# Halves of 128 tokens for the first FFN products of two units, and a wider choice of engine for conversions, in a local-attention and FFN kernel

## The chip, the cores and the metric

The kernel runs on one core of a Trainium2 chip. The core has TensorE (PE in the profile, its weight loads PEld), VectorE (DVE), ScalarE (ACT), GpSimd (POOL) and SyncE (SP), which here only issues DMAs. The metric is the device time of one execution in microseconds (us), lower is better.

## The reference

Attention over 4 batches, 8 heads, 768 tokens and 64 dimensions, in which each token sees its neighbours within 15 positions and, beside them, 24 block summaries (the maximum of the keys and the mean of the values of 32 tokens each); then an FFN over the 3072 resulting rows.

```python
k_sum = k.reshape(B, H, nb, 32, D).max(axis=3)
v_sum = v.reshape(B, H, nb, 32, D).mean(axis=3)
scores_l = where(|pos_i - pos_j| < 16, q @ k.T / sqrt(D), -1e9)
scores_s = q @ k_sum.T / sqrt(D) + log(32)
a = softmax(concat(scores_l, scores_s))          # over 768 + 24 keys
x = (a @ concat(v, v_sum)) as rows (3072, 512)
h = x @ w_in                                      # (3072, 2048)
g = h * sigmoid(h)
out = g @ w_out                                   # (3072, 512), float32
```

The inputs q and k are random with a spread of 0.8, v of 0.1. The FFN weights arrive as 64-bit floats.

## The kernel before, in words

**Tiling.** The 3072 rows are 24 stages of 128 tokens. Two stages make one chunk of 256 tokens, 12 chunks in all. The hidden dimension of 2048 is cut into 8 slices of 256, called f or fp. One FFN **unit** is a chunk with a slice; there are 96, numbered in the order in which they are worked (units 0 to 3 are chunk 0 with slices 0 to 3, units 4 to 7 chunk 1 with the same, then slices 4 to 7 of chunk 1, then of chunk 0, then the later chunks whole).

**A unit** (`job_f`) has two first products (`ffn1`, L904 to L908, d = 0 and 1), each 12 matmuls of 128x128 weights against 256 tokens, since x and the weights are held as a high and a low f16 part and three of the four cross terms are formed. Their result is in a PSUM bank h: 0 or 1 for the first chunks. Then ScalarE takes the tanh (L922), VectorE forms (t + 1) * h (L923), ScalarE casts that to f16 as gh (L927), and GpSimd or VectorE forms the rest gl = t - gh (L928, through the helper at L276). The first eight units that use slices 0 to 3 for chunks 0 and 1 are "plain": they have one scaled f32 copy g (L925) and no rest. The second products (L917) follow, 6 matmuls of 512 columns for each of the two halves of the tokens.

**A stage** (`job_a`, `job_c`, `job_x`): scores of two heads in one group (L671 for stages 0 to 3 in f32, L674 for 4 and 5, L676 and L677 later), a row minimum on VectorE (L688), the exponential with its sum on ScalarE (L691). In stages 0 to 3 the f32 exponentials are transposed on TensorE (L700, L702), copied out of PSUM by ScalarE or VectorE (L705), and multiplied with the values (L746, the AV product). A small product broadcasts the reciprocal sums (L791), VectorE multiplies (L795), and xh and xl, the two f16 parts of x, are formed (L797, L798). Later stages normalize first (L713, L715, L717), write two f16 parts, transpose them by DMA (L729) and multiply at L762.

**Weights** (`job_w`): each slice of w_in and w_out comes as 1 MB by DMA (L816), is rebuilt to f32 out of its two 32-bit words (L818 to L828), its largest value is found (L838, or as a bound by sums on ScalarE at L836 and L840), turned into a power of two with a small product (L848, L852), and split in two f16 parts: the high one on ScalarE (L860), the low one on VectorE (L861). The values' scale of batch 0 comes from VectorE maxima over six tiles (L603) in `job_mean`, which also forms the block means (L600).

**What sets the order.** Every operation is recorded in a `Plan` with the engines on which it may run, its cost there, and what it reads and writes. `ORDER` is a string in the program: each three characters, read to base 36, are the operation's number times five plus an engine's number (L182). `replay` (L178) runs through it, and the instructions of each engine are put out in that order; each engine works strictly in it. Since the list is plain text, it can be decoded by reading it against the numbers in which the program records its operations. Operations with the "port" mark on VectorE and GpSimd are kept from overlapping in the plan, and long GpSimd ones get a wait on the VectorE one before (L241).

**Fillers.** Where `replay` expects TensorE to stand idle early on, it puts in products of 256 columns with the identity (L389) that write to bank 0 and are not used. They end for good with the first operation that is entered with 3072 columns or more (L197), and that is the first `ffn1`.

**Queues.** All DMAs go out on SP, in their own order of `ORDER`.

Of the kernel before, what the change touches and what calls it, by code (L numbers as in the profile page):

```python
# [14 lines left out]
AF = mybir.ActivationFunctionType  # L15
ALU = mybir.AluOpType
# [5 lines left out]
P = 128  # L22
# [28 lines left out]
APART = 2  # L51
NSUP = 2
# [199 lines left out]
def local_attn_ffn(ctx: ExitStack, tc: tile.TileContext, q0, qkT, qF, qD, kF, kD, v, vR, w, out):  # L252
# [289 lines left out]
    def job_qk(s, prio):  # L542
# [22 lines left out]
        plan.op({"act": 1040}, lambda e: nc.scalar.activation(out=qh, in_=qr, func=AF.Copy, scale=qs[:, 0:1]), r=key + sc, w=[("qk", s % 2, hp) for hp in range(4)], prio=prio)  # L565
# [4 lines left out]
        plan.op({"act": 1240}, lambda e: nc.scalar.activation(out=kst[:, :, :NLOC], in_=kr, func=AF.Copy, scale=qs[:, 1:2]), r=key2 + sc, w=[("qkk", s % 2)], prio=prio)  # L570
# [16 lines left out]
    def job_mean(prio):  # L587
        prio += nudge("mean")
        k = sbank()
        for t in range(NTILE):  # L590
# [11 lines left out]
            if NPL < NTILE:  # L602
                plan.op({"dve": 603}, lambda e, src=src, t=t: nc.vector.tensor_reduce(out=am_t[:, t:t + 1], in_=src, axis=AX.X, op=ALU.max, apply_absolute_value=True), r=key, w=[("am", t)], prio=prio, port=())  # L603
# [5 lines left out]
    def job_vs(s, prio):  # L609
# [12 lines left out]
        def vm(e):  # L622
            for u in range(2):
# [3 lines left out]
        plan.op({"act": 1040, "pool": 1097}, lambda e: nc.scalar.activation(out=vr, in_=vr, func=AF.Copy, scale=vsc[:, 0:1]) if e == "act" else  # L627
                nc.gpsimd.tensor_scalar(out=vr, in0=vr, scalar1=vsc[:, 0:1], scalar2=0.0, op0=ALU.mult, op1=ALU.add), r=[("vsc", b % 2)], w=key, prio=prio)
# [141 lines left out]
    def job_x(s, prio):  # L770
# [7 lines left out]
        if s < NPL:  # L778
# [18 lines left out]
            plan.op({"act": 560}, lambda e: nc.scalar.copy(out=xh, in_=xr3), r=[("xr", s % 2)], w=[("xh", z, half)], prio=prio)  # L797
# [59 lines left out]
    def split_w(fp, kind, by, need, prio):  # L857
        wf = plain_w[fp, kind].rearrange("p j c -> p (j c)")
        hi, lo = (wt[fp, kind][:, i].rearrange("p j c -> p (j c)") for i in range(2))
        plan.op({"act": 1050}, lambda e: times(e, hi, wf, by), r=[("wv", fp, kind)] + need, w=[("wp", fp, kind), ("wh", fp, kind)], prio=prio)  # L860
# [29 lines left out]
    def job_f(i, c, f):  # L890
# [13 lines left out]
        def ffn1(d):  # L904
            def go(e):
                for ct in range(NCT):
                    for q, (part, x) in enumerate(((0, xh), (0, xl), (1, xh))):
                        nc.tensor.matmul(out=h[:, d * CH:(d + 1) * CH], lhsT=wt[f, 0][:, part, d, ct * P:(ct + 1) * P], rhs=x[:, ct, :], start=(ct == 0 and q == 0), stop=(ct == NCT - 1 and q == 2))  # L908
            return go
# [10 lines left out]
        for d in range(2):  # L920
# [3 lines left out]
        if plain:  # L924
            plan.op({"act": 600}, lambda e: times(e, g, t, ur_t[:, f, 0:1]), r=[("t", j), ("ur", f)], w=[("gh", n), ("gl", n)], prio=at - TUNE["post"])  # L925
# [245 lines left out]
```

## Time and profile before

| | |
|---|---|
| Median of 3 runs | 612.52 us (612.44 to 612.62) |
| Profiled execution | 612.63 us |
| its span, first to last instruction | 610.9 us |
| TensorE busy | 605.8 us, 99% |
| VectorE, ScalarE, GpSimd busy | 466.9, 391.5, 139.7 us |
| granted TensorE clock | 0.999 |
| DMA | 93.50 MB, mean 153 GB/s |

The span is what the trace shows, from the first instruction to the last; the rest of the execution's time, 1.7 us, lies around it. A product counts as busy from its issue until its modelled end, so that two in a row overlap: the step from one start to the next, not the length, is what a product costs in a row of them.

### The profile page before, as it was taken

To read this page: it belongs to the slowest core of one execution; us is meant where nothing else is said; L and a number is where in the kernel's file an instruction comes from. 1 tells how busy PE (TensorE), PEld (TensorE's weight loads), DVE (VectorE), ACT (ScalarE), POOL (GpSimd) and SP (SyncE) were. 2 spreads that over 40 slices of the span, in tenths; PEclk is the share of its full clock that TensorE was granted. 3 is DMA by queue.
4 is the path that set the end of the run, shared out by engine and by line. 5 is a ranking of instruction groups with operands and counts; after the bars stand their busy time and mean duration, and the time that the engine had idled before them with its cause. 6 is when DMAs were issued, how large, how long until landed. Compare 5 with 4: busy or idle time off the path is not lost.

```text
span 610.9 us, 13765 instructions
## 1 busy us (share of the span) xinstructions
PE 605.8 (99%) x5085; PEld 427.6 (70%) x5085; DVE 466.9 (76%) x1384; ACT 391.5 (64%) x866; POOL 139.7 (23%) x172
## 2 busy tenths in 40 slices
PE   8999999999999999999999999999999999999997
PEld 5786756677676776767777676767767667666785
DVE  7998978999889766897888846997788876753321
ACT  3999989667776667655787567644665655442222
POOL 2333321023314301413303341112422012101000
PEclk9999999999999999999999999999999999999999
DMA  8999615764666754583775764685565652502100
GB/s 310 342 335 382 248 40 167 172 158 114 191 137 141 202 172 142 158 210 82 195 145 130 173 194 136 152 197 124 98 161 130 143 131 64 87 14 57 53 2 35
DMA packets 91560, 93.50 MB, mean 153 GB/s; under 512 B 70348, under 2 KB 72652, under 8 KB 89444
## 3 DMA queue, kind: packets, MB, share of 16 engines
q1 hardware_dynamic: 91492, 92.62, 56.0%
q8 instruction: 40, 0.66, 0.5%
q14 instruction: 28, 0.23, 0.1%
HBM read 68.12 MB, written 6.29 MB: 122 GB/s over the span
## 4 chain that ended last, share of the span: by engine, by line
PE 94%; DMA 3%; ACT 1%; SPq 0%; DVE 0%; issue 0%
PE bank L917 42%; PE bank L908 41%; PE bank L762 4%; PE bank L676 2%; PE bank L677 2%; DMA wt<-in_w_dram 1%; DMA wt<-in_kF_dram 1%; PE bank L746 1%; DMA wt<-vms 1%; PE bank L674 1%; PE bank L671 0%; ACT wt L826 0%; ACT e L691 0%; PE bank L389 0%; PE bank L460 0%
## 5 line engine op out<-in xcount | busy, mean ns | idle before, releaser
L917 PE MATMUL bank<-wt,g 128*128 128x512 f16 (+2 forms) x1168 | 278.6, 382 | 0.0
L908 PE MATMUL bank<-xh,wt 128*128 128x256 f16 x1536 | 273.9, 273 | 0.0
L908 PEld LDWEIGHTS <-wt 128*128 128x128 f16 x2304 | 224.1, 98 | 45.1 <-issue 3.3
L908 PE MATMUL bank<-xl,wt 128*128 128x256 f16 x768 | 209.3, 273 | 0.0
L917 PEld LDWEIGHTS <-g 128*128 128x128 f16 x1104 | 106.7, 98 | 95.3 <-issue 0.8
L922 ACT ACTIVATE t<-bank,asc 128x512 f32<-128x512 f32 x96 | 65.7, 684 | 90.0 <-PE bank L908 89.7
L923 DVE SCALAR_TENSOR_TENSOR t<-t,bank 128x512 f32<-128x512 f32 x96 | 65.5, 683 | 55.7 <-ACT t L922 55.1
L691 ACT ACTIVATE e<-e,mx 128x182 f32<-128x182 f32 x192 | 83.8, 438 | 29.2 <-DVE mx L688 28.9
L927 ACT CAST g<-t 128x512 f16<-128x512 f32 x88 | 54.1, 615 | 49.4 <-DVE t L923 46.3
L726 DVE SCALAR_TENSOR_TENSOR p<-e,sum,p 128x128 f16<-128x128 f32 x320 | 80.1, 313 | 2.9 <-POOL p L715 1.7
L276 POOL TENSOR_TENSOR g<-t,g 128x512 f16<-128x512 f32 x31 | 35.9, 1158 | 161.3 <-ACT g L927 77.5
L688 DVE CUSTOM_DVE_ANT_0 e<-bank,masks,qsc 128x182 f32<-128x182 f32 x144 | 54.0, 402 | 21.0 <-PE bank L677 19.0
L715 POOL TENSOR_SCALAR p<-e,sum 128x182 f16<-128x182 f32 x45 | 24.6, 549 | 119.1 <-DVE sum L708 23.5
L276 DVE TENSOR_TENSOR g<-t,g 128x512 f16<-128x512 f32 x57 | 39.7, 696 | 12.0 <-ACT g L927 11.3
L691 ACT ACTIVATION_READ_ACCUMULATOR e<-e,mx 128x1 f32 x192 | 36.1, 188 | 0.0
L713 ACT ACTIVATE p<-e,sum 128x182 f16<-128x182 f32 x65 | 26.6, 437 | 14.1 <-DVE sum L708 7.4
L276 POOL TENSOR_TENSOR vv<-raw,vv 128x1024 f16<-128x1024 f32 x12 | 25.6, 2133 | 15.6 <-DVE p L717 5.9
L571 DVE SCALAR_TENSOR_TENSOR qk<-raw,qsc,qk 64x1264 f16<-64x1264 f32 x18 | 27.6, 1535 | 2.0 <-ACT qk L570 1.4
L676 PE MATMUL bank<-qk 128*128 128x182 f16 x144 | 28.7, 241 | 0.0
L677 PE MATMUL bank<-qk 128*128 128x182 f16 x144 | 28.7, 242 | 0.0
L570 ACT ACTIVATE qk<-raw,qsc 128x1264 f16<-128x1264 f32 x18 | 24.1, 1340 | 5.1 <-DMA raw<-in_kD_dram 5.1
L566 DVE SCALAR_TENSOR_TENSOR qk<-raw,qsc,qk 128x1024 f16<-128x1024 f32 x18 | 23.7, 1316 | 3.7 <-ACT qk L565 3.6
(169 smaller groups left out, 640.1 us busy)
## 6 DMA issues: line engine op xcount, KB each, us to landing
wt<-in_w_dram SPq DMA_DIRECT2D x16, 1024.0 KB
raw<-in_kD_dram SPq DMA_DIRECT2D x18, 632.0 KB
raw<-in_v_dram SPq DMA_DIRECT2D x20, 512.0 KB
raw<-in_qD_dram SPq DMA_DIRECT2D x18, 512.0 KB
out_dram<-raw SPq DMA_DIRECT2D x23, 256.0 KB
raw<-in_kF_dram SPq DMA_DIRECT2D x12, 384.0 KB
raw<-in_qF_dram SPq DMA_DIRECT2D x9, 512.0 KB
raw<-in_vR_dram SPq DMA_DIRECT2D x12, 384.0 KB
```

The costliest lines, as they stand in the source:

```text
L276: eng[e].tensor_tensor(out=out, in0=in0, in1=in1, op=ALU.subtract)
L571: plan.op({"dve": 1450}, lambda e: nc.vector.scalar_tensor_tensor(out=kst[64:, :, :NLOC], in0=kr[64:], scalar=qs[64:, 1:2], in1=kst[64:, : ...
L676: nc.tensor.matmul(out=sc[:, i, :NKEY], lhsT=qh[:, h, :], rhs=kst[:, h, :], start=True, stop=False)
L677: nc.tensor.matmul(out=sc[:, i, :NKEY], lhsT=ql[:, h, :], rhs=kst[:, h, :], start=False, stop=True)
L688: plan.op({"dve": 258 if b == 0 else 323}, lambda e, i=i: nc.vector.tensor_tensor_reduce(out=et[:, i, :NKEY], in0=sc[:, i, :NKEY], in1=mas ...
L691: plan.op({"act": 431}, lambda e, i=i, h=h: nc.scalar.activation(out=et[:, i, :NKEY], in_=et[:, i, :NKEY], func=AF.Exp, scale=-1.0, bias=m ...
L726: nc.vector.scalar_tensor_tensor(out=pt[:, i, to:to + z - a], in0=et[:, i, a:z], scalar=su[:, i:i + 1], in1=pt[:, i, a:z], op0=ALU.mult, o ...
L908: nc.tensor.matmul(out=h[:, d * CH:(d + 1) * CH], lhsT=wt[f, 0][:, part, d, ct * P:(ct + 1) * P], rhs=x[:, ct, :], start=(ct == 0 and q == ...
L917: nc.tensor.matmul(out=bank[to][:, :z0 - a0], lhsT=a[:, d * CH + u * P:d * CH + u * P + P], rhs=b[:, d, a0:z0], start=(opens and d == 0 an ...
L922: plan.op({"act": 640}, lambda e: nc.scalar.activation(out=t, in_=h, func=AF.Tanh, scale=asc_t[c // 3 % 2][:, f:f + 1]), r=[("bank", k), ( ...
L923: plan.op({"dve": 605}, lambda e: nc.vector.scalar_tensor_tensor(out=t, in0=t, scalar=1.0, in1=h, op0=ALU.add, op1=ALU.mult), r=[("bank", ...
L927: plan.op({"act": 540}, lambda e: nc.scalar.copy(out=gh, in_=t), r=[("t", j)], w=[("gh", n)], prio=at - TUNE["post"])
```

## The change

It has three parts, and a new `ORDER` (2532 entries in place of 2528).

**1. Halves.** For units 0 and 1 (chunk 0, slices 0 and 1) each of the two first products is made in two operations of 128 tokens each. One reads only the xh and xl of its own half of the chunk, that is, of one stage. There are eight operations of 12 matmuls with 128 columns where there were four of 12 with 256. Each is entered in the plan with 3072 columns, as a whole one.

**2. ScalarE may bound the values' scale by sums.** The reductions at L603 may run on ScalarE as a sum of absolute values, scaled by 2^-7, which writes its unused result to a buffer of the FFN. In the new order two of six do.

**3. Conversions may change engine.** Seven kinds of operation that had ScalarE alone, or ScalarE and GpSimd, may run on ScalarE, GpSimd or VectorE. What the new order makes of it, decoded:

| operation | count | moved |
|---|---|---|
| g cast to gh (L927) | 88 | 27 to GpSimd, 29 to VectorE |
| plain g (L925) | 8 | 3 to GpSimd, 2 to VectorE |
| high part of the weights (L860) | 16 | 7 to GpSimd |
| q (L565), k (L570) | 18 each | 2 and 3 to GpSimd, 1 and 2 to VectorE |
| xh of the first stages (L797) | 4 | 2 to GpSimd, 1 to VectorE |
| rest gl (L928) | 88 | 16 from GpSimd to VectorE, 13 the other way |
| scaled v (L627), its rest (L630) | 20 each | 6 from GpSimd to ScalarE and 2 to VectorE; 7 from GpSimd to VectorE |
| scaled exponentials (L713, L715, L717) | 160 | 102 change among the three |

In all VectorE has 958 operations instead of 926, ScalarE 594 instead of 642, GpSimd 164 instead of 148.

```diff
+HALVED = 2
@@ job_qk, split_w and others alike
-        plan.op({"act": 1040}, lambda e: nc.scalar.activation(out=qh, in_=qr, func=AF.Copy, scale=qs[:, 0:1]), ...)
+        plan.op({"act": 1040, "pool": 1110, "dve": 650}, lambda e: times(e, qh, qr, qs[:, 0:1]), ...)
@@ job_mean
+                def bound(e, src=src, t=t):
+                    if e == "act":
+                        nc.scalar.activation(out=t_t[t % NT2], in_=src, func=AF.Abs, scale=2.0 ** -7, accum_out=am_t[:, t:t + 1])
+                    else:
+                        nc.vector.tensor_reduce(out=am_t[:, t:t + 1], in_=src, axis=AX.X, op=ALU.max, apply_absolute_value=True)
+                plan.op({"dve": 603, "act": 620}, bound, r=key, w=[("am", t), ("t", t % NT2)], prio=prio, port=())
@@ job_f
-        def ffn1(d):
+        def ffn1(d, half=None):
+            a0, z0 = (0, CH) if half is None else (half * P, half * P + P)
...
-                        nc.tensor.matmul(out=h[:, d * CH:(d + 1) * CH], lhsT=..., rhs=x[:, ct, :], ...)
+                        nc.tensor.matmul(out=h[:, d * CH + a0:d * CH + z0], lhsT=..., rhs=x[:, ct, a0:z0], ...)
...
+        early = c == 0 and f < HALVED
+        for half in range(2 if early else 0):
+            for d in range(2):
+                plan.op({"pe": 690}, ffn1(d, half), r=[(x, z, half) for x in ("xh", "xl")] + ..., cols=3072)
+        for d in range(0 if early else 2):
...
-            plan.op({"act": 540}, lambda e: nc.scalar.copy(out=gh, in_=t), ...)
+            plan.op({"act": 540, "pool": 590, "dve": 345}, lambda e: copy(e, gh, t), ...)
```

TensorE's order around the first units, decoded (s is the stage, u the unit, "turn" the transposes of two heads, "sums" L791, "AV" L746, "gather" L848):

```
before: scores s2a | sums s1 | AV s1 | turn turn | gather | sums s2 | scores s3a | AV s2 |
        u0 d0 | turn turn | u0 d1 | scores s3b | u1 d0 | u1 d1 | second products of u0 ...
after:  sums s1 | scores s2a | gather | AV s1 | turn | u0 d0 tokens 0-127 | turn | sums s2 |
        u0 d1 tokens 0-127 | scores s3a | AV s2 | u0 d0 tokens 128-255 | turn turn |
        u0 d1 tokens 128-255 | u1 d0 tokens 0-127 | scores s3b | u1, three more | second products of u0 ...
```

(Here s2a stands for the second score group of stage 2, s3a and s3b for the two of stage 3.) The other orders are new throughout as well. On SP the first weights of slice 0 stand two places earlier, the last tile of v for the block means three places later.

More of the change, by code (lines that the diff above doesn't have):

```diff
@@ L564, in job_qk @@
         plan.op({"dma": 1360}, lambda e: nc.sync.dma_start(out=stg[:, :H * P], in_=qD[b - 1, t]), w=key, prio=prio)
-        plan.op({"act": 1040}, lambda e: nc.scalar.activation(out=qh, in_=qr, func=AF.Copy, scale=qs[:, 0:1]), r=key + sc, w=[("qk", s % 2, hp) for hp in range(4)], prio=prio)
+        plan.op({"act": 1040, "pool": 1110, "dve": 650}, lambda e: times(e, qh, qr, qs[:, 0:1]), r=key + sc, w=[("qk", s % 2, hp) for hp in range(4)], prio=prio)
         plan.op({"dve": 1200}, lambda e: nc.vector.scalar_tensor_tensor(out=ql, in0=qr, scalar=qs[:, 0:1], in1=qh, op0=ALU.mult, op1=ALU.subtract), r=key + sc, w=[("qk", s % 2, hp) for hp in range(4)], prio=prio)
@@ L626, in job_vs @@
         plan.op({"dma": 480}, vm, r=["vms"], w=key, prio=prio, cols=1520)
[L627 to L628 removed]
+        plan.op({"act": 1040, "pool": 1097, "dve": 650}, lambda e: times(e, vr, vr, vsc[:, 0:1]), r=[("vsc", b % 2)], w=key, prio=prio)
         plan.op({"dve": 602, "act": 950, "pool": 1014}, lambda e: copy(e, v1, vr), r=key, w=[("v1", j), ("v1", j, "side")], prio=prio)
@@ L796, in job_x @@
             xr3 = xr.rearrange("p (c t) -> p c t", c=NCT)
-            plan.op({"act": 560}, lambda e: nc.scalar.copy(out=xh, in_=xr3), r=[("xr", s % 2)], w=[("xh", z, half)], prio=prio)
+            plan.op({"act": 560, "pool": 590, "dve": 345}, lambda e: copy(e, xh, xr3), r=[("xr", s % 2)], w=[("xh", z, half)], prio=prio)
             plan.op({"dve": 680, "pool": 1280}, lambda e: less(e, xl, xr3, xh), r=[("xr", s % 2), ("xh", z, half)], w=[("xl", z, half)], prio=prio)
@@ L907, in go @@
                     for q, (part, x) in enumerate(((0, xh), (0, xl), (1, xh))):
-                        nc.tensor.matmul(out=h[:, d * CH:(d + 1) * CH], lhsT=wt[f, 0][:, part, d, ct * P:(ct + 1) * P], rhs=x[:, ct, :], start=(ct == 0 and q == 0), stop=(ct == NCT - 1 and q == 2))
+                        nc.tensor.matmul(out=h[:, d * CH + a0:d * CH + z0], lhsT=wt[f, 0][:, part, d, ct * P:(ct + 1) * P], rhs=x[:, ct, a0:z0], start=(ct == 0 and q == 0), stop=(ct == NCT - 1 and q == 2))
             return go
@@ L918, in ffn2 @@
             return go
-        for d in range(2):
+        early = c == 0 and f < HALVED
+        for half in range(2 if early else 0):
+            for d in range(2):
+                plan.op({"pe": 690}, ffn1(d, half), r=[(x, z, half) for x in ("xh", "xl")] + [("wh", f, 0), ("wl", f, 0)] + ([("turn", i - APART)] if i >= APART else []), w=[("bank", k)], prio=at + nudge("f1", i), cols=3072)
+        for d in range(0 if early else 2):
             plan.op({"pe": 1310}, ffn1(d), r=[(x, z, half) for x in ("xh", "xl") for half in range(2)] + [("wh", f, 0), ("wl", f, 0)] + ([("turn", i - APART)] if i >= APART else []), w=[("bank", k)], prio=at + nudge("f1", i), cols=3072)
```

137 lines of the change are left out of this document (68 added, 69 removed).

## The prediction, before the run

> **What bounds the kernel now.** I read the page first, then the windows by stage, then the timeline of single instructions between 20 and 46 us. The page:
>
> ```profile
> span 610.9 us, 13765 instructions
> PE 605.8 (99%) x5085; PEld 427.6 (70%) x5085; DVE 466.9 (76%) x1384; ACT 391.5 (64%) x866; POOL 139.7 (23%) x172
> ...
> PE 94%; DMA 3%; ACT 1%; SPq 0%; DVE 0%; issue 0%
> ```
>
> TensorE is the bound: it is busy for 605.8 of 610.9 us and carries 94% of the chain that ended last. Time can therefore only come out of what TensorE does that is not the computation, or out of its gaps. The windows (length, then busy us of each engine with its instruction count, clock, DMA share, GB/s) say where that is:
>
> ```profile
> 6.00:21.00 15.00, 14.66 (x105) 8.57 (x104) 13.01 (x48) 10.52 (x38) 1.16 (x1) 1.00 1.02 374
> 21.00:28.00 7.00, 6.80 (x91) 6.03 (x91) 6.79 (x26) 6.71 (x17) 2.53 (x2) 1.00 0.89 290
> ...
> 39.00:600.00 561.00, 561.00 (x4669) 396.55 (x4668) 431.53 (x1251) 359.06 (x784) 127.10 (x147) 1.00 0.55 143
> ```
>
> From 39 to 600 us no gap is recorded. But busy is not useful: L389, the filler product that keeps the array working, counts as busy too. The same windows, for L389 alone:
>
> ```profile
> 21.00:28.00 7.00, 1.21 (x10) 1.04 (x11) 1.00 0.89 290
> 28.00:33.00 5.00, 0.61 (x4) 0.14 (x2) 1.00 1.02 410
> 33.00:36.00 3.00, 1.86 (x14) 1.30 (x14) 1.00 0.72 210
> 36.00:611.00 575.00, 0.00 (x0) 0.00 (x0) 1.00 0.54 142
> ```
>
> After 21 us every filler lies before 36 us (those ahead of 21 are the opening run, until the first scores can start). What they stand in for is seen in TensorE's timeline (start, length, line, shape, count):
>
> ```profile
> 27.18 1.15 PE L389 MATMUL bank<-ident 128*128 128x256 bf16 x9
> 28.25 0.55 PE L671 MATMUL bank<-wt,qk 64*128 64x158 f32 x4
> ...
> 33.39 0.60 PE L389 MATMUL bank<-ident 128*128 128x256 bf16 x4
> 33.91 0.64 PE L791 MATMUL bank<-unit,sh 128*64 128x128 f16 x16
> 34.48 1.27 PE L389 MATMUL bank<-ident 128*128 128x256 bf16 x10
> 35.68 0.55 PE L671 MATMUL bank<-wt,qk 64*128 64x158 f32 x4
> ...
> 36.79 2.12 PE L746 MATMUL bank<-wt 128*64 128x128 f32 x32
> 38.84 0.28 PE L908 MATMUL bank<-xh,wt 128*128 128x256 f16 x1
> ```
>
> From filler start to next real start: 28.25 − 27.18 = 1.07, 33.91 − 33.39 = 0.52 and 35.68 − 34.48 = 1.20 us, 2.79 us in three places. That is nearly all there is to win. TensorE waits here for the early attention stages (tokens 0 to 511), whose chain runs through ScalarE and VectorE, and the FFN cannot fill the holes because its first instruction (38.84) reads both token halves of chunk 0.
>
> **The change part by part.** (1) The halves. What they need is ready earlier:
>
> ```profile
> 26.98 1.27 DVE L273 SCALAR_TENSOR_TENSOR wt<-wt,ur 128x1024 f16<-128x1024 f32 x1
> ...
> 39.74 1.27 DVE L273 SCALAR_TENSOR_TENSOR wt<-wt,ur 128x1024 f16<-128x1024 f32 x1
> ```
>
> ```profile
> 29.65 1.16 POOL L276 TENSOR_TENSOR xl<-xr,xh 128x512 f16<-128x512 f32 x1 [0.15 <-ACT xh L797]
> ...
> 36.48 1.17 POOL L276 TENSOR_TENSOR xl<-xr,xh 128x512 f16<-128x512 f32 x1 [1.96 <-DMA raw<-vms]
> ```
>
> Weights of unit 0 are split by 26.98 + 1.27 = 28.25 and tokens 0 to 127 by 29.65 + 1.16 = 30.81; tokens 128 to 255 only by 37.65, and unit 1's weights by 41.01. So exactly two half products, those of unit 0 over tokens 0 to 127, can run in the holes, and the decoded new order places exactly these two ahead of the scores that started at 35.68 and of the AV product (L746 at 36.79): the first between two transposes, the second between L791 and the scores.
>
> Their price. Twelve 256-column products take 1.31 us (24 in 2.73, with overlap at the end); the weight loads in between and the smaller shape nearest to the new one:
>
> ```profile
> 43.62 2.73 PE bank L908 x24
> ```
>
> ```profile
> 181.56 2.42 PE L762 MATMUL bank<-tt,vv 128*64 128x128 f16 x80
> ```
>
> ```profile
> L908 PEld LDWEIGHTS <-wt 128*128 128x128 f16 x2304 | 224.1, 98 | 45.1 <-issue 3.3 <-DVE wt L828 0.3 <-POOL raw L628 0.2
> ```
>
> No row shows a 128-column product with 128 new weight columns. Lower bound: half of 109 ns (1.31/12), 55 ns, 0.66 us for twelve. Upper bound: the whole 98 ns of a weight load, were none overlapped, 1.18 us. L762 loads 64 weight columns for each of its 128-column products and two of them cover the array: 2 × 2.35/80 = 59 ns, 0.70 us for twelve (2.35 is 2.42 without the tail that the next instruction overlaps). I take 0.70. Behind AV, units 0 and 1 then need six halves, 6 × 0.70 = 4.20, where four whole ones stood, 4 × 1.31 = 5.24: −1.04 us (bounds 6 × 0.66 − 5.24 = −1.28 and 6 × 1.18 − 5.24 = +1.84).
>
> [...]
>
> (2) Where the AV product ends. It is behind the scores at 35.68, which wait for banks 4 and 5 to be copied out. Here the engine choices act: one of the two copies that ScalarE ran in a row (the 27.18 hole) goes to VectorE, the broadcast product L791 for stage 1 moves into that hole, and VectorE, 13.01 of 15 and 6.79 of 7 us busy in the windows above, loses two of these reductions to ScalarE:
>
> ```profile
> 16.52 1.27 DVE L603 TENSOR_REDUCE am<-wt 128x1 f32<-128x512 f32 x2
> ```
>
> as well as one 1.2 us maximum of unit 1's weights. Against that, ScalarE is itself full from 28 us on, and the first half product delays the transpose behind it, which frees bank 4. Bounds: gain at most what the holes hold beyond the two halves, 2.79 − 1.40 = 1.39; loss at most one half product, 0.70. I take −0.5: the copy in parallel saves about 0.5 us in the 1.07 us hole, and the rest of the chain neither gains nor loses.
>
> (3) Conversions to f16 that leave ScalarE: 56 of the 88 casts of g (27 to GpSimd, 29 to VectorE), 7 of 16 weight splits to GpSimd, a few of q, k, v and x. Prices:
>
> ```profile
> L262 DVE CAST vv<-raw 128x1024 f16<-128x1024 f32 x3 | 2.1, 691 | 1.4 <-ACT raw L627 1.4
> ```
>
> ```profile
> L260 POOL TENSOR_SCALAR vv<-raw 128x1024 f16<-128x1024 f32 x10 | 10.5, 1046 | 33.7 <-DVE g L276 16.0 <-ACT xh L266 8.8 <-DVE qk L566 5.1
> ```
>
> At half the size a g cast is about 0.35 to 0.42 us on VectorE and 0.52 to 0.63 on GpSimd. On ScalarE it is 0.62, seen with its whole chain at the end of the kernel:
>
> ```profile
> 600.14 0.69 ACT L922 ACTIVATE t<-bank,asc 128x512 f32<-128x512 f32 x1 [1.22 <-PE bank L908]
> 600.86 0.69 DVE L923 SCALAR_TENSOR_TENSOR t<-t,bank 128x512 f32<-128x512 f32 x1 [1.14 <-ACT t L922]
> 601.63 0.62 ACT L927 CAST g<-t 128x512 f16<-128x512 f32 x1 [0.81 <-DVE t L923]
> 602.28 0.69 DVE L276 TENSOR_TENSOR g<-t,g 128x512 f16<-128x512 f32 x1 [0.74 <-ACT g L927]
> ```
>
> The chain takes 602.97 − 600.14 = 2.83 us, 3.1 with its start. TensorE covers it with other work: first and second products stream 3072 columns alike, 1.31 us, and a score group of 728 columns by the same rate 0.31. In the new order the shortest cover is then 2 × 1.31 + 2 × 0.31 = 3.2 us (unit 16, both steps on VectorE: 3.1 − 0.62 + 0.4 = 2.9 needed); for a unit with both steps on GpSimd it is 4.2 (unit 12: 2 × 1.31 and two f32 score groups of some 0.8, below the 1.11 us of the larger group at 35.68; 3.1 − 0.62 + 0.6 − 0.69 + 1.16 = 3.6 needed). So I cost part 3 at nothing; without that cover it costs what the chain is late, as the third rival prices. VectorE gains 32 instructions net; it was 431.53 of 561 us busy.
>
> (4) The DMA order: unit 0's first weights go two places earlier, the last mean tile three later; the count is the same. The DMA engines are full until 21 us (1.02), so it only shifts landings. I cost it at nothing, between −0.5 and +0.3 (the sizes of the gaps at 6 to 28 us, 0.34 + 0.20).
>
> Sum: −1.04 − 0.5 = −1.5 us. The profiled execution took 612.63 (610.9 plus 1.7 around it), the median 612.52: 612.5 − 1.5 = **611.0 us**, 0.25% faster. A difference under 0.2%, 1.2 us, cannot be told from no change here.
>
> **The rivals.** *Everything is recovered.* VectorE's relief also pulls the whole early chain forward and all 2.79 us go, with the gaps of 0.54: 612.5 − 2.79 − 0.54 + 0.35 (eight halves at 0.70 against four at 1.31) = 609.5. For it: VectorE is 97% busy at 21 to 28 us. Against: the transfer of the block means and ScalarE, not VectorE alone, set those stages.
>
> *The holes only move.* TensorE takes its instructions in order; a half product that waits holds the transpose and the scores behind it, so bank 4 is freed later, its copies later, the next scores later. If each half delays that chain by its own 0.70, AV ends 1.40 later and the −1.04 is gone: 612.5 to 612.9. For it: xl of half 0 now passes three GpSimd steps (weight split, xh, xl), before only xl. Against: 30.81 leaves some 1 us before the first half product can start.
>
> *GpSimd is held up by VectorE, and the second products wait (slower).* The row that speaks for it:
>
> ```profile
> 25.16 1.35 POOL L268 TENSOR_SCALAR asc<-ur,vsc 128x1 f32<-128x1 f32 x1
> ```
>
> ```profile
> 25.25 1.21 DVE L828 SCALAR_TENSOR_TENSOR wt<-wt 128x1024 uint32<-128x1024 uint32 x1
> ```
>
> One element took 1.35 us on GpSimd, just as long as the VectorE instruction beside it. By the same count three units with both steps on GpSimd have 4.2, 4.6 and 4.6 us of cover (units 12, 58, 83) for 3.6. One hold of 1.2 us costs them 0.6 + 0.2 + 0.2 = 1.0; two holds cost 1.8 + 1.4 + 1.4, and two more units with 5.0 and 5.6 of cover 1.0 and 0.4, together 6.0. Between them, 3.5: 612.5 − 1.5 + 3.5 = 614.5. It decides where a hold exceeds the 0.6 us of spare cover. Against it: GpSimd ran such steps before too (29.65 above), and TensorE had no gap from 39 to 600 us.
>
> [...]
>
> *Weight loads set the pace of the halves*: +1.84 in place of −1.04, 613.8. Against it: 59 ns at L762.
>
> *The clock drops.* No filler can be issued once the first half product is out. At half clock for 3.4 us of work, 1.7 us are lost: 612.7. Against it: the windows show a granted clock of 1.00 with fillers at 12 to 62% of a stretch, and in the stretch without them two halves, two transposes, L791, scores and AV leave holes under 1 us.
>
> [...]
>
> **How the numbers follow.** Forecast 0.42, everything recovered 0.13, holes only move 0.22, GpSimd held up 0.15, weight loads 0.05, clock 0.03. The forecast's own range is 610.2 to 611.9, from −0.5 ± 0.8 in part 2. Leaving out half of the first rival's side below and two thirds of the GpSimd case above, 80% lie in 609.6 to 613.4. Faster by 0.2% (under 611.3): most of the forecast, 0.36, and all of the first rival, 0.13, with 0.02 of the others: 0.51. Same (611.3 to 613.7): 0.06 + 0.20 + 0.03 + 0.03 = 0.32. Slower: 0.17.
>
> **What would show it.** Two half products of about 0.70 us ahead of the AV product, fewer than ten fillers after 28 us, and the AV product ending near 38.3: parts 1 and 2. No TensorE wait on g after 40 us: part 3. A half product well over 0.8 us, a granted clock under 1.00, or waits of the second products on GpSimd would each make it wrong by the rival that names it.

## The result and the profile after

Slower. The changed kernel takes 616.32 us (median of 8, 613.97 to 618.30) against 612.64 for the kernel before: ratio 1.0055, 95% interval 1.0037 to 1.0074. The prediction was 611.0 with a range of 609.6 to 613.4. On a second chip (run e10 below) it is 614.47 against 612.81, 1.0027 [1.0013, 1.0041]. The chips differ by less for the kernel before (612.6 to 613.0 throughout), so below each kernel is compared with the runs of before made beside it. One number needs a word more: in five of these eight executions the mean granted clock is 0.997 or less (0.996 in the profiled one, which dips between 28 and 32 us), and these are in the medians.

The page of the changed kernel, profiled execution 618.3 us. It is the slowest of the eight, so the profile of e10, the same kernel at 615.73 us and without a dip of the clock, is set beside it where the two differ:

```profile
span 616.6 us, 13824 instructions
PE 606.4 (98%) x5114; PEld 427.3 (69%) x5114; DVE 490.2 (80%) x1416; ACT 360.6 (58%) x821; POOL 130.7 (21%) x188
...
PE 84%; DMA 8%; DVE 3%; SPq 2%; issue 1%; ACT 1%; POOL 1%; ACTq 0%; POOLq 0%; DVEq 0%
```

TensorE's idle time has doubled, from 610.9 − 605.8 = 5.1 to 10.2 us, and the chain that ended last now runs 8% through DMAs, where it had 3%. Windows (length, busy of each engine with its count, clock, DMA share, GB/s) say where:

```profile
6.00:21.00 15.00, 14.15 (x103) 8.23 (x102) 12.45 (x48) 11.24 (x42) 1.17 (x1) 1.00 0.99 362
21.00:28.00 7.00, 5.95 (x82) 4.92 (x80) 5.45 (x23) 5.22 (x12) 1.34 (x2) 1.00 0.87 327
28.00:33.00 5.00, 5.00 (x48) 3.73 (x49) 3.40 (x8) 3.92 (x8) 3.32 (x5) 0.66 1.03 347
39.00:100.00 61.00, 59.34 (x456) 41.14 (x454) 54.26 (x110) 56.45 (x96) 22.22 (x31) 1.00 0.62 222
400.00:500.00 100.00, 98.09 (x829) 68.38 (x827) 85.44 (x260) 54.01 (x133) 17.15 (x26) 1.00 0.57 135
```

Between 21 and 28 us TensorE is idle for 1.05 us (0.20 before), and ScalarE and VectorE, busy 6.71 and 6.79 of those 7 us before, now 5.22 and 5.45: they stand still too. The clock then falls to 0.66 for 5 us, 5 × 0.34 = 1.7 us of work; in windows of 0.5 us it is 0.52 from 28.5 us, 0.50 from 29 to 31.5, 0.56 from 31.5 and 1.00 from 32 on. Further on TensorE has gaps of 1.66 and 1.91 us, where it had none. Its waits, by line and releaser (us in total, times, longest):

```profile
PE bank L925 <- POOL g L269: 1.7, 1, 1.7
PE bank L925 <- POOL g L277: 1.7, 1, 1.7
```

In e10 these two are 1.2 and 0.5 us, and there is one of 0.8 us for a query tile.

**The first place: up to 41 us.** The loads on SyncE's queue, before and then after:

```profile
10.29 0.33 SPq L816 DMA_DIRECT2D wt<-in_w_dram  x1
...
12.50 0.33 SPq L548 DMA_DIRECT2D qk<-in_q_dram  x1
12.87 1.01 SPq L816 DMA_DIRECT2D wt<-in_w_dram  x2
```

```profile
8.54 0.33 SPq L822 DMA_DIRECT2D wt<-in_w_dram  x1
12.75 0.33 SPq L549 DMA_DIRECT2D qk<-in_q_dram  x1
13.12 0.43 SPq L598 DMA_DIRECT2D wt<-in_v_dram  x1
...
14.99 0.43 SPq L822 DMA_DIRECT2D wt<-in_w_dram  x1
```

The queue stands still from 8.87 to 12.75 us. At its head is the query tile of stage 2 for the second two head pairs, whose buffer is free only when the second scores of stage 0 are done. In before that load went out at nearly the same time, 12.50, but the last value tile and the other query tile were out by then, and the next two weight slices followed at once, at 12.87. Now they all stand behind it, and the slice of w_out for unit 0 goes out at 14.99, in before at 13.45. It lands hardly later for that: the last of its load's signals stands at 24.83 in this trace and at 24.57 in before's. What has changed is who waits for it, in the timeline of the changed kernel:

```profile
24.86 1.18 ACT L832 ACTIVATE wt<-wt 128x1024 f32<-128x1024 f32 x1 [1.78 <-DMA wt<-in_w_dram]
24.86 0.70 DVE L830 TENSOR_SCALAR wt<-wt 128x1024 uint32<-128x1024 uint32 x1 [1.48 <-DMA wt<-in_w_dram]
...
26.40 0.44 ACT L697 ACTIVATE e<-e,mx 128x182 f32<-128x182 f32 x1
...
39.12 2.12 PE L752 MATMUL bank<-wt 128*64 128x128 f32 x32
41.17 0.23 PE L916 MATMUL bank<-xh,wt 128*128 128x128 f16 x1
```

Two instructions of that slice now stand ahead of stage 2 in the orders of ScalarE and VectorE: L832 ahead of its exponentials, L830 ahead of its row minima. Both wait until 24.83 for the transfer, and all behind them wait too. The exponentials start at 26.40; before:

```profile
23.78 0.45 ACT L691 ACTIVATE e<-e,mx 128x182 f32<-128x182 f32 x1
```

So 2.62 us late, and the AV product of stage 2 ends at 41.17 in place of 38.84. In before this slice's L826 stood behind those exponentials, and its last bits were read on GpSimd at 28.34, with time to spare.

The 2.33 us at the AV product have two parts. In six other profiles with the slice in this place (e2, e3, e9, e10, e13, e16) AV ends 13.4 to 13.5 us behind the start of the exponentials, which would be about 39.85 here: some 1.0 us goes with the late exponentials, the other 1.3 with the stretch at a clock of 0.66. In e10, without a dip, the exponentials start at 26.85 and AV ends at 40.30, 1.46 later than in before.

**The second place: 47 us.** The second product of unit 0 waits for g:

```profile
45.51 1.16 POOL L828 TENSOR_SCALAR wt<-wt 128x1024 uint32<-128x1024 uint32 x1 [5.03 <-PE bank L677]
46.70 1.23 DVE L834 SCALAR_TENSOR_TENSOR wt<-wt 128x1024 uint32<-128x1024 uint32 x1
46.75 1.65 POOL L261 TENSOR_SCALAR xh<-xr 128x512 f16<-128x512 f32 x1
48.38 0.69 POOL L269 TENSOR_SCALAR g<-t,ur 128x512 f32<-128x512 f32 x1
49.12 1.12 PE L925 MATMUL bank<-wt,g 128*128 128x512 f32 x2 [1.66 <-POOL g L269]
```

Its input t was ready at 45.68. On GpSimd there stand ahead of it another slice's last bits (L828: this row names a product as what it waited for last, the profiles of e1, e9, e10 and e11 the slice's load) and xh of stage 2, which takes 1.65 us; VectorE's L834 runs beside it from 46.70 to 47.93.

**The third place: 467 to 473 us.** The same pattern with a key tile:

```profile
468.19 1.35 ACT L267 ACTIVATE qk<-raw,qsc 128x1264 f16<-128x1264 f32 x1 [4.12 <-DMA raw<-in_kD_dram]
469.45 0.60 ACT L259 CAST g<-t 128x512 f16<-128x512 f32 x1
469.58 1.53 DVE L572 SCALAR_TENSOR_TENSOR qk<-raw,qsc,qk 64x1264 f16<-64x1264 f32 x1 [3.29 <-ACT qk L267]
...
471.29 1.16 POOL L277 TENSOR_TENSOR g<-t,g 128x512 f16<-128x512 f32 x1 [6.32 <-DVE qk L572]
...
472.50 1.04 PE L925 MATMUL bank<-wt,g 128*128 128x512 f16 x4 [1.65 <-POOL g L277]
```

ScalarE stands 4.12 us before a load, with unit 70's cast behind it, and GpSimd's rest of g waits in turn for VectorE.

### The profile page after: what moved, and what is told of

Read it like the earlier page. It is cut to its first block, busy times and chain, and to the rows that moved or that the text cites. A ratio compares the mean times of both kernels' runs of the same rounds, so it can differ in the third digit from the quotient of the medians.

```text
span 616.6 us, 13824 instructions
## 1 busy us (share of the span) xinstructions
PE 606.4 (98%) x5114; PEld 427.3 (69%) x5114; DVE 490.2 (80%) x1416; ACT 360.6 (58%) x821; POOL 130.7 (21%) x188
## 4 chain that ended last, share of the span: by engine, by line
PE 84%; DMA 8%; DVE 3%; SPq 2%; issue 1%; ACT 1%; POOL 1%; ACTq 0%; POOLq 0%; DVEq 0%
PE bank L925 38%; PE bank L916 36%; PE bank L768 3%; DMA wt<-in_w_dram 3%; DMA raw<-in_v_dram 2%; PE bank L682 2%; PE bank L683 2%; DMA raw<-in_kD_dram 1%; DMA wt<-in_kF_dram 1%; DMA raw<-vms 1%; DMA tt<-p 1%; PE bank L752 1%; PE bank L677 1%; DVE vv L277 1%; PE bank L680 1%
## 5 line engine op out<-in xcount | busy, mean ns | idle before, releaser
L925 PE MATMUL bank<-wt,g 128*128 128x512 f16 (+2 forms) x1168 | 277.7, 383 | 3.3 <-POOL g L269 1.7
L916 PE MATMUL bank<-xh,wt 128*128 128x256 f16 (+1 forms) x1568 | 274.2, 270 | 0.0
L916 PE MATMUL bank<-xl,wt 128*128 128x256 f16 (+1 forms) x784 | 210.6, 270 | 0.2 <-DVE xl L274 0.2
L925 PEld LDWEIGHTS <-g 128*128 128x128 f16 x1104 | 106.5, 98 | 98.7 <-POOL g L277 2.6
L277 POOL TENSOR_TENSOR g<-t,g 128x512 f16<-128x512 f32 x28 | 32.5, 1162 | 89.6 <-DVE g L263 23.5
L277 DVE TENSOR_TENSOR g<-t,g 128x512 f16<-128x512 f32 x60 | 41.6, 693 | 11.6 <-POOL g L261 8.6
L719 ACT ACTIVATE p<-e,sum 128x182 f16<-128x182 f32 x81 | 33.6, 439 | 26.7 <-DVE sum L714 13.3
L261 POOL TENSOR_SCALAR g<-t 128x512 f16<-128x512 f32 x27 | 16.7, 619 | 146.7 <-DVE t L935 92.6
L267 ACT ACTIVATE qk<-raw,qsc 128x1024 f16<-128x1024 f32 (+1 forms) x28 | 34.3, 1234 | 13.8 <-DMA raw<-in_kD_dram 10.0
L721 POOL TENSOR_SCALAR p<-e,sum 128x182 f16<-128x182 f32 x40 | 17.6, 444 | 102.0 <-DVE sum L714 33.3
L259 ACT CAST g<-t 128x512 f16<-128x512 f32 x32 | 19.7, 615 | 13.3 <-DVE t L935 12.9
L768 PEld LDWEIGHTS <-vv 128*64 128x64 f16 x800 | 22.8, 110 | 3.2 <-issue 2.5
```

The source lines that it names most:

```text
L267: nc.scalar.activation(out=out, in_=in_, func=AF.Copy, scale=by)
L277: eng[e].tensor_tensor(out=out, in0=in0, in1=in1, op=ALU.subtract)
L768: nc.tensor.matmul(out=to[j * D:(j + 1) * D, i * P:(i + 1) * P], lhsT=vs[w][:, vi, h * D:(h + 1) * D], rhs=tt[:, j * 3 + blk, :], start=(n ...
L916: nc.tensor.matmul(out=h[:, d * CH + a0:d * CH + z0], lhsT=wt[f, 0][:, part, d, ct * P:(ct + 1) * P], rhs=x[:, ct, a0:z0], start=(ct == 0 ...
L925: nc.tensor.matmul(out=bank[to][:, :z0 - a0], lhsT=a[:, d * CH + u * P:d * CH + u * P + P], rhs=b[:, d, a0:z0], start=(opens and d == 0 an ...
```

## The experiments

All keep what the kernel computes. But for e5, each has the changed program; the edits are to the written-out order, shown decoded. "Stage 2" below is its row minima, exponentials and copies; "slice B" the second kind of unit 0's weights, the one that lands at 24.83; A is the first kind of unit 0's weights, C that of unit 1's.

**e1, e11, e8: slice B behind stage 2.**

```diff
 ScalarE
-  slice B (L832) | copy m5 | exponentials m8, m9 | ... | copies m8, m4 | xr s1
+  copy m5 | exponentials m8, m9 | ... | copies m8, m4 | xr s1 | slice B (L832)
-VectorE: last bits of slice B (L830) | row minima m8, m9
+GpSimd:  last bits of slice B (L828) | high part of unit 0's weights (L866)
```

> The changed kernel with two instructions of one weight slice (unit 0, second kind) moved in the written-out order: its ScalarE conversion (L832) behind the exponentials and copies of stage 2 instead of ahead of them, its last-bits step (L830) from VectorE, ahead of the row minima of stage 2, to GpSimd (L828), behind them. Nothing else of the order changes; six more fillers come with it. Theory Q (an instruction that waits for a late transfer holds its whole engine): the exponentials of stage 2 start near 24.3 us instead of 26.40, its AV product starts near 37 instead of 39.12, the granted clock stays 1.00 in 28 to 33 us, and the time falls by the 2.3 us that the AV product was late, and by about 1.5 more where the clock had dropped: 612.8 to 614.3. Rival U (the exponentials are late because of what is upstream of the slice, the later query and value tiles): the start stays near 26 and the time near 616.3. Rival C (only the clock drop costs): the time falls by 1.5 or less, 614.8 or more, whatever becomes of the exponentials.

612.79 against 612.65, 1.0005 [0.9991, 1.0020]: the time that theory Q gave. The profile bears it out in part. The exponentials start at 24.60 and the clock stays at 1.00, but AV starts at 38.08, not near 37, with a wait of 0.9 us for a query tile on the way, and ends at 40.12. And the chip was another than that of the changed kernel's first runs, and with the move came six more fillers (34 in place of 28). So it was run once more without them:

> The kernel of the first run with exactly the identity products of the changed kernel (28, at the same places) in place of its 34. It tells whether the first run gained by the two moved instructions or by the six identity products that came with them. Theory Q (the moved instructions alone): 612.4 to 613.0. Rival F (the identity products keep the clock up): the clock drops below 1.00 in the stretch behind 28 us and the time is 614.0 or more.

616.09 against 612.69, 1.0046 [1.0031, 1.0062], on a third chip. This looked like rival F. But its profile loses time before the first place at which its fillers differ from those of e1, which is at about 23 us: from 8 to 12 us the clock is at 0.52 and 0.63 (rows below, under the hardware), SyncE's standing load goes out at 13.74, in e1 at 12.54, and slice B follows at 15.99 in place of 14.78. So both kernels and the changed one went to one chip:

> The changed kernel unchanged, beside the others on one chip, since two runs with nearly the same order (the first and the one with fewer identity products) came out 3.3 us apart on two chips. 616.3 if the chip plays no part.

> The first run's kernel again on the same chip as the changed one. Theory Q: 612.8, 3.5 under the changed kernel. Rival V (its gain was the draw of one chip, on which the slice happened to land early): within 1 us of the changed kernel, and its profile shows the slice landing no later than 22.5 where it is quick and behind 23 where it is slow.

Changed kernel 614.47, 1.0027 [1.0013, 1.0041]; slice moved 613.50, 1.0012 [0.9998, 1.0027]. On equal terms the move is worth about 1.0 us, not 3.5, and the two intervals overlap. Theory Q holds for a part. Rival V fits by its number (within 1 us), but not by what it wanted of the landing: the slice landed at 25.36 in e1, the quick run, and at 24.83 in the changed kernel's slow one. In e11's profile the loads went out later than in any other (slice B at 16.74, landing at 25.91), and that execution was still faster than the changed kernel's (614.47 against 615.73). Whether the six fillers matter is open, since no two runs on one chip differ by them alone.

**e6, e9, e12: the loads of before.**

```diff
 SyncE, first loads (v2 to v5: value tiles, q s2: a query tile of stage 2)
-  ... v2 v3 v4 q s1 q s1 | A | q s2 | v5 | side v | C | q s2 | B | q s3 ...
+  ... q s1 v2 v4 q s1 v5 side v v3 | A | q s2 | side v | q s2 | C | B | q s3 ...
```

> The kernel of the first run (slice's conversion behind the exponentials) with the first 22 loads of SyncE's queue in the order of the kernel before (one query tile of stage 3 behind them). The prediction costed the new order of the loads at nothing, -0.5 to +0.3. Theory D (the new order of the loads costs): TensorE's waits for query tiles, value tiles and copied key sums in the first 28 us (1.1 us in the first run's profile) go, and the time falls by 0.6 to 1.1 under that run, 611.7 to 612.2. Rival N: it is worth nothing, 612.6 to 612.9.

612.88 against 612.69, 1.0017 [0.9992, 1.0041]. Nine of its twelve executions are between 611.16 and 613.03; the other three, at a granted clock of 0.994 to 0.997, over 616.9. The profiled execution (611.52) is the first that took less than before's 612.63: its waits behind the opening are 0.8 us for a value tile, and nothing else.

> The changed kernel with only the order of SyncE's first 22 loads put back to that of before; the slice's conversion stays ahead of the exponentials. Theory D (root: the new load order puts a query tile of stage 2, whose buffer is free only when the scores of stage 0 are done, ahead of a value tile and three weight slices, so the queue stands still and every later load is late): the slice lands near 21 us instead of 24.83, ScalarE and VectorE no longer wait for it, the AV product of stage 2 starts near 37, and the time falls by 3 or more to 612 to 613.3. Rival Q (the place of the slice's conversion is the cause by itself): the slice still lands behind 23, the time stays over 615.

614.43, 1.0028 [1.0014, 1.0042]: the same as the changed kernel beside it (614.47). By the median theory D falls as a cause by itself. Its mechanism held in part: in this profile (613.30) the exponentials start at 25.63 and AV starts near 37 as it said, at 37.05, and ends at 39.10; 1.3 us then go in a wait for g of unit 0. What it said of the landing did not hold: slice B goes out at 13.49, but

```profile
24.09 1.20 ACT L832 ACTIVATE wt<-wt 128x1024 f32<-128x1024 f32 x1 [0.77 <-DMA wt<-in_w_dram]
24.09 0.70 DVE L830 TENSOR_SCALAR wt<-wt 128x1024 uint32<-128x1024 uint32 x1 [0.45 <-DMA wt<-in_w_dram]
```

it takes over 10 us to land. So it does in before (13.45 to 24.57), where nobody waited for it. By the medians it takes both: a slice that lands so late must not stand ahead of stage 2, and the loads must not stand behind a wait.

> The kernel with the slice's conversion moved and the loads in the order of before (it was 611.2 to 613.0 in nine of twelve executions, at granted clock 1.00, and 617.0 to 618.6 in three, at 0.994 to 0.997), with five more identity products ahead of the first column sum of the value tiles, where TensorE stands idle from 7.05 to 8.17 us. Theory C (that idle time is what sometimes lowers the clock): every execution at 0.999 or 1.00 and a median of 611.5 to 612.8, no execution over 614. Rival (the clock drops elsewhere): executions at 0.997 or less remain.

615.26, 1.0046 [1.0026, 1.0066]. Not what theory C said: one execution of seven at 0.997, the rest at 0.999 and 1.00, and the median still over that of e6. The profile shows waits of 1.6 us for g of unit 0 and 1.3 us for a late unit, the second and third place. What the five fillers did to these, if anything, is open.

**e2, e3, e4, e13: the second and the third wait.**

```diff
 e2, GpSimd
-  last bits of unit 2's slice (L828) | xh s2 (L261) | g u0 (L269) | last bits
+  g u0 (L269) | last bits of unit 2's slice (L828) | xh s2 (L261) | last bits
 e3, ScalarE and GpSimd
-  key tile (L267) | gh u70 (L259);  gl u70 (L277) behind the key tile's L572
+  gh u70 (L259) | key tile (L267);  gl u70 (L277) ahead of it
 e13
-  GpSimd: xh s2 | g u0 (L269)
+  VectorE: (t + 1) * h (L935) | g u0 (L271)
```

> The changed kernel with GpSimd's plain conversion of unit 0's activations (g, L269) moved ahead of two other GpSimd steps that stand before it in the order: the last bits of a weight slice (L828), which wait for a transfer, and the conversion xh of stage 2 (L261). Theory Q: g is done near 46.6 us, TensorE's idle 1.66 us at 47.4 us goes, and the time falls by 1.7 to 614.6. Rival S (the stall is soaked up: the two delayed steps make a wait of the same size later): TensorE's wait at 47 us goes and another takes its place within 20 us, the time stays near 616.3.

> The changed kernel with the two conversions of one late unit (chunk 8, unit 6: gh on ScalarE, gl on GpSimd) moved ahead of the conversion of a key tile (L267 on ScalarE, L572 on VectorE) whose transfer lands at 468.2 us. Theory Q: TensorE's two waits at 467 to 473 us (1.9 us together) go, and the time falls by 1.9 to 614.4. Rival S: the key tile's own users are then late by as much, a wait stands at their score product, and the time stays near 616.3.

> The three moves together. Theory Q with stalls that add: 2.0 to 3.5, 1.7 and 1.9 us come back, 609.2 to 610.7, under the kernel before. If the stall at 47 us is only a consequence of the first delay, two of the three add and the time is 610.9 to 612.4. Rival S or U: over 614.

On one chip with e1: e2 615.36, 1.0034 [1.0019, 1.0048]; e3 615.58, 1.0044 [1.0028, 1.0060]; e4 613.87, 1.0023 [1.0010, 1.0037], which is 1.1 us over e1 (612.79) though it has two moves more. The waits named go in the profiles. In e2 others stand in their place, 1.1 us for a value tile and 0.4 us for the maximum of unit 2's slice (L854 <- DVE wm L856), in e4 0.9 us at that same L854, whose slice the move holds up: rival S for the second place. In e3 none as long took the place of the third; but its ratio lies between the two of the changed kernel, and e1, with the old order there, has no such wait in its profile. That wait comes and goes with the loads, and e3 is inconclusive.

> The changed kernel with unit 0's plain conversion g on VectorE, right behind the step that makes its input, in place of GpSimd; all else as it is. Theory P (GpSimd's conversion, held by the transfer ahead of it and by VectorE beside it, costs the wait of 1.2 to 1.7 us at 47 us): no wait of TensorE for g of unit 0, and 1.0 to 1.7 us less than the changed kernel, 0.0 to 0.3% over before. Rival S (what is late behind it, the weight slice of unit 2 and the second products' other inputs, takes its place): less than 0.5 us less, 0.2% or more over before.

614.68, 1.0031 [1.0019, 1.0043]. No wait for g in its profile, and beside 1.0027 and 1.0055 for the changed kernel on two other chips no gain that could be told. Whether removing that wait gives anything stays open.

**e5, e7, e17: halves and whole products.**

> The kernel before with one part of the change alone: the first products of units 0 and 1 in halves of 128 tokens, everything else in the order of before. Unit 0's two products on the first half stand in the two holes behind the transposes of stage 2 and ahead of the scores of stage 3, where before had identity products; the six other halves stand where the four whole products stood. Theory H (the halves are worth what their sum says): six halves at 0.67 us in place of four products at 1.31 are 1.2 us less on TensorE's full stretch, 611.4 to 611.8. Rival M (the holes only move: what follows waits for VectorE and ScalarE as before): 612.4 to 612.9.

612.62 against 612.69, 1.0007 [0.9994, 1.0020]: rival M. Its profile (613.46) shows how the gain is taken back. AV ends at 38.22, 0.62 us ahead of before (0.44 of that stood already at 27 us, ahead of the halves), TensorE then waits 0.47 us for a VectorE copy at 41.26, the second products of unit 0 start at 45.31, 0.88 ahead, and the next AV product at 50.40, 0.41 ahead; the rest is lost behind 140 us. Its diff to the kernel before is the halves of the change, and in TensorE's order `turn | u0 d0 tokens 0-127 | turn | sums s2 | u0 d1 tokens 0-127 | scores s3a`, the rest halves where the whole ones stood.

> The kernel of the first run with the first products of units 0 and 1 whole again, each at the place of the half that completes it; every other engine's order is the same, and the holes are filled with identity products (51 in place of 34). Theory H: 1.0 to 1.2 us more than that run, 613.8 to 614.0. Rival M: the halves are worth nothing in this order either, 612.6 to 612.9.

615.81, 1.0046 [1.0034, 1.0059], on e5's chip. Three us more than e1, but that was on another chip; e8, with the slice moved and the halves in, took 616.09 on this one. With the early loads late, it told nothing of the halves.

The run that could tell came last, when the early loads and the late part (below) no longer disturbed:

```diff
-HALVED = 2
+HALVED = 0
 TensorE
-  turn | u0 d0 0-127 | turn | sums s2 | u0 d1 0-127 | scores s3a | AV s2 | u0 d0 128-255 | ...
+  turn | 8 fillers | turn | sums s2 | 9 fillers | scores s3a | AV s2 | u0 d0 | ...
```

> The kernel with the slice's conversion moved, the early loads in the order of before and the order of before from 104 us on, with the first products of units 0 and 1 whole again, each at the place of the half that completes it, and 52 identity products in place of 35. Theory H (step one of the prediction): 1.0 to 1.2 us more than with halves, 0.12 to 0.20% over before, 613.5 to 613.7 where before is 612.7. Rival M (the holes only move): as with halves, -0.1 to 0.05% against before.

> The kernel with the slice's conversion moved, the early loads in the order of before, g of unit 0 on VectorE and the order of before from 104 us on, halves in. If the gains add: 0.10 to 0.25% under before, 611.2 to 612.1 where before is 612.7. If what was gained early is held by what comes behind 46 us: as without g's move, -0.05%, 612.4.

Both on one chip, before 612.76: whole products 612.94, 1.0000 [0.9987, 1.0013]; halves (and g of unit 0 on VectorE) 612.11, 0.9986 [0.9970, 1.0001]. That is 0.83 us, the profiled executions 612.63 and 611.63. The intervals overlap, but nine of the twelve executions with halves are below the fastest with whole products (612.58). In their timelines, e17 first:

```profile
33.29 1.04 PE L390 MATMUL bank<-ident 128*128 128x256 bf16 x8
34.26 0.64 PE L797 MATMUL bank<-unit,sh 128*64 128x128 f16 x16
34.83 1.16 PE L390 MATMUL bank<-ident 128*128 128x256 bf16 x9
...
37.03 2.11 PE L752 MATMUL bank<-wt 128*64 128x128 f32 x32
39.07 0.28 PE L916 MATMUL bank<-xh,wt 128*128 128x256 f16 x1
...
46.42 1.88 PE L925 MATMUL bank<-wt,g 128*128 128x512 f32 x4
```

```profile
33.19 0.22 PE L916 MATMUL bank<-xh,wt 128*128 128x128 f16 x1
...
33.80 0.22 PE L916 MATMUL bank<-xh,wt 128*128 128x128 f16 x1
34.40 0.64 PE L797 MATMUL bank<-unit,sh 128*64 128x128 f16 x16
34.97 0.23 PE L916 MATMUL bank<-xh,wt 128*128 128x128 f16 x1
...
36.96 2.12 PE L752 MATMUL bank<-wt 128*64 128x128 f32 x32
39.01 0.23 PE L916 MATMUL bank<-xh,wt 128*128 128x128 f16 x1
...
45.15 1.94 PE L925 MATMUL bank<-wt,g 128*128 128x512 f32 x4
```

The halves take exactly the place of the fillers, AV ends where it ended (39.07 and 39.01), and behind it six halves stand for four whole products. From there to the second products of unit 0 (the last row of each) it is 46.42 − 39.07 = 7.35 us with whole products and 45.15 − 39.01 = 6.14 with halves, 1.21 less. This shows the halves' gain as far as g's place is left aside; e17 kept g on GpSimd, without a wait in its profile.

**e14, e15, e16: early against late.** e14 is e6 with g of unit 0 on VectorE. e15 is e6 up to 104 us and from there on the engines and the order of before; e16 the changed kernel up to 104 us, then the same.

> The slice's conversion moved, the loads in the order of before and g of unit 0 on VectorE. If the losses up to 41 us and at 47 us are the two early ones, work done at 60 us stands 1.0 to 1.4 us ahead of before in its profile, and the time is 611.3 to 612.6 unless a late wait is added to it. If either was not: within 0.5 us of before at 60 us.

> The slice's conversion moved and the loads in the order of before up to 104 us, and from there on the engines and the order of the kernel before for everything. Theory L (the conversions' new engines and order behind 104 us cost 0.3 to 2.6 us, by late loads in front of GpSimd's steps): no wait of TensorE behind 104 us, 0.3 to 1.0 us less than with the late part of the changed kernel, 611.3 to 612.3. Rival E (the loss is all early): as the sixth run, 612.9.

> The changed kernel up to 104 us, and from there on the engines and the order of the kernel before. Theory L: no wait of TensorE behind 104 us, 0.5 to 1.5 us less than the changed kernel, 0.1 to 0.3% over before. Rival E: as the changed kernel, 0.3 to 0.5% over before.

On one chip, with e13 beside them, before 612.95:

| | early loads and slice B | late part | median | ratio |
|---|---|---|---|---|
| e13 | changed | changed | 614.68 | 1.0031 [1.0019, 1.0043] |
| e16 | changed | before | 615.12 | 1.0034 [1.0015, 1.0052] |
| e14 | before's loads, B moved | changed | 612.17 | 0.9996 [0.9984, 1.0009] |
| e15 | before's loads, B moved | before | 612.45 | 0.9995 [0.9984, 1.0007] |

The two early edits are worth 2.5 and 2.7 us, the late part nothing: rival E, by the medians. Some of this goes with the clock: its mean is 0.997 or less in one of e13's eight executions and six of e16's twelve, in none of e14 and e15. Among the others the medians of e13 and e14 are still 2.4 us apart, those of e16 and e15 only 0.8. In single executions theory L is seen all the same. To follow one, I sum the products recorded up to a time, each at the step from start to start that its shape shows in before, fillers left out, and take how many us later (+) than in before the same sum is reached; one profiled execution each, good to about 0.2 us:

| | at 46 us | 60 us | 250 us | the end |
|---|---|---|---|---|
| changed kernel | +1.0 | +2.6 | +2.8 | +5.6 |
| e10, the same | +0.4 | +1.6 | +1.7 | +3.0 |
| e16 | −1.8 | −0.1 | +0.2 | +0.2 |
| e14 | −1.0 | −0.6 | −0.3 | +2.9 |
| e15 | −1.4 | −1.6 | −0.9 | −0.9 |
| e17 | +0.2 | 0.0 | 0.0 | 0.0 |
| e18 | −1.2 | −1.4 | −1.1 | −1.1 |

With the late part of the changed kernel an execution can lose 1.3 to 3.2 us behind 250 us (e14's profile was its slowest, 615.61 of a median 612.17), though the profiles of e6, e9 and e13 lost nothing of that size there; with that of before none of the four profiled did. In e16 slice B happened to land early,

```profile
23.37 1.19 ACT L832 ACTIVATE wt<-wt 128x1024 f32<-128x1024 f32 x1 [0.55 <-DMA wt<-in_w_dram]
```

AV ended at 38.44, 0.40 ahead of before, and it was 1.8 us ahead at 46 us, until the wait for g took that back; this execution took 612.94, seven of the twelve of the same kernel over 614.7, all but one of these with a dip of the clock. The changed order is not slow as such. It is close, and pays when a load is late or the clock dips.

## Why the prediction was wrong, step by step

**What bounds the kernel** was right: what can be won lies before 41 us and is some 2.8 us; e18's profiled execution won 1.0 of it.

**Part 1, the halves: right in price, and in size where the rest of the order lets them be.** The price was 0.70 us for a half product. In the changed kernel (its first and last of twelve):

```profile
35.34 0.22 PE L916 MATMUL bank<-xh,wt 128*128 128x128 f16 x1
...
35.95 0.22 PE L916 MATMUL bank<-xh,wt 128*128 128x128 f16 x1
```

0.61 us for eleven steps, 55.5 ns each, 0.67 us for twelve, and that with a new weight load for each product (twelve of 98 ns, beside the products). The sum is then 6 × 0.67 − 5.24 = −1.22 in place of −1.04, and e17 against e18 shows −1.21 on the stretch itself, −1.0 by profiles and −0.83 by medians. In the order of before (e5) the same halves gave nothing: there *the holes only move* held.

**Part 2, "I take −0.5 … the rest of the chain neither gains nor loses": this failed.** AV ended at 41.17, 2.33 us later than before, beyond the bound of +0.70. The bounds counted what the change does on TensorE and to the copies; they left out that the new orders of ScalarE and VectorE set two steps of slice B ahead of stage 2. About 1.0 of the 2.33 goes with the exponentials that this made late, 1.3 with the dip of the clock; e10, without a dip, was 1.46 late, beyond the bound too. With the slice moved and the loads put back (e6, e12, e14, e15, e17, e18) AV ends at 38.72 to 39.17, between 0.1 earlier and 0.3 later than before: the gain of 0.5 did not come there. Once, in e16, when the slice landed early, 0.40 of it did. (The forecast's own range, by −0.5 ± 0.8, ends at 611.8 and not at 611.9.)

**Part 4, "it only shifts landings. I cost it at nothing": this failed with it.** The count of loads and the full DMA engines were looked at, not what the load at the queue's head waits for, nor who waits for what lands. The text even listed two moved loads and missed the third, the query tile that stops the queue. It was not slice B that the new order of loads made late (24.83, in before 24.57); what it held up shows in TensorE's waits for other loads between 6 and 46 us, those of query tiles and values: with slice B moved they are 1.1 to 2.2 us in the four profiles with the new order of loads (e1, e4, e8, e11) and 0.0 to 0.8 in the six with that of before (e6, e12, e14, e15, e17, e18). Neither failure is the whole: by medians the slice's place alone is worth about 1.0 us (e11 against e10), the loads alone 0.0 (e9 against e10), both together 2.5 to 2.7 (e14, e15 against e13, e16), or 0.8 to 2.4 among executions without a dip. Why the two do not add up stays open.

**Part 3, "I cost part 3 at nothing": nearly right by the medians, wrong in kind.** The table of cover asked for each unit how long its own chain takes. The waits of 1.7 us came where another step ahead on the same engine had to wait (units 0 and 70), not at units 12, 58 and 83. Taking one away gave nothing measurable (e13), and so did the late part as a whole (e16 against e13); in single executions it cost 1.3 to 3.2 us.

**The rivals.** GpSimd held up (614.5, 0.15) has its rows now: 1.65 us for a conversion of 0.62, beside VectorE's L834. But taking the conversion off GpSimd gave nothing that could be told (e13), so that is not shown to be where the median went. The clock rival gave 1.7 us for 3.4 us at half clock. Before's profile has no such stretch; the changed kernel's has one, with the clock at 0.50 from 28.5 to 31.9 us. But its condition was wrong. It wanted a stretch without fillers behind the first half product; the dip came before that product, after a stretch in which TensorE waited for the late exponentials. Weight loads setting the pace is refuted at 55.5 ns.

**Of the marks set out beforehand**, fillers after 28 us (3) and the half product (0.67) came as forecast; AV near 38.3, no wait on g and a clock of 1.00 did not.

## What to carry to other kernels

When an order written out by hand or by a model changes, walk each engine's new queue and ask of every entry that waits for a load: when did that load really land in the trace, and what stands behind the entry. Here a slice that lands at 23 to 26 us in the traces was harmless behind stage 2 in the kernel before; ahead of stage 2, and with other loads behind a waiting query tile, it cost the change its gain. A local saving can be right in size and still be outweighed by where its schedule put unrelated work; measure the part by itself before the whole is judged.

## What the runs showed of the hardware

**A granted clock of 0.50 to 0.63 after 0.71 and 1.05 us of idle time, and of 1.00 after 1.66.** In e8, windows of 2 us on TensorE (busy with count, clock, DMA share, GB/s):

```profile
6.00:8.00 2.00, 1.29 (x16) 1.00 1.01 329
8.00:10.00 2.00, 2.00 (x3) 0.52 1.01 391
10.00:12.00 2.00, 2.00 (x7) 0.63 1.10 406
```

0.71 us of idle time between 6 and 8 us were followed by windows at 0.52 and 0.63; in the changed kernel 1.05 us between 21 and 28 were followed by the 0.66 above, while the 1.66 us at 47 us, between the half products and those of 512 columns, left it at 1.00 (46 to 50 us), and so did 1.34 and 1.65 us between 20 and 28 us in e10 and e3 (1.00 from 28 to 33). What the granted clock goes by in such a stretch was not settled.

**A GpSimd conversion of 0.62 or 0.70 us took 1.65 beside VectorE's L834, and in another run it was L834 that took longer.** For xh it was 0.62 at 29.42 us and 1.65 at 46.75 in the changed kernel. In e9, g:

```profile
44.54 1.57 DVE L834 SCALAR_TENSOR_TENSOR wt<-wt 128x1024 uint32<-128x1024 uint32 x1
45.02 1.65 POOL L269 TENSOR_SCALAR g<-t,ur 128x512 f32<-128x512 f32 x1
```

and in e1, where GpSimd was first:

```profile
45.55 0.70 POOL L269 TENSOR_SCALAR g<-t,ur 128x512 f32<-128x512 f32 x1
45.67 1.64 DVE L834 SCALAR_TENSOR_TENSOR wt<-wt 128x1024 uint32<-128x1024 uint32 x1
```

In these two runs the one that began later took longer: g 1.65 in place of 0.70, L834 1.64 in place of 1.22, its median in the changed kernel (its 1.57 in e9 stands behind an xh that GpSimd had begun at 44.43).

**A load of 1 MB took over 10 us.** Slice B went out at 13.49 in e9, landed at 24.07 and was first read at 24.09, while the mean busy share of the DMA engines was 1.05 from 8 to 20 us, 0.85 from 20 to 24 and 0.94 from 24 to 28.
